# State columns side by side in `vs` from the third batch on

## The chip, the cores and the metric

One core of a Trainium2 chip runs the whole kernel in one launch. The metric is device time in microseconds of one execution; before the change it was 651.02 us, the median of 3 runs (648.34 to 651.56). The profile is of one further execution, which took 647.52 us.

## The reference

Three layers follow each other, all in float32, for 4 batches, 8 heads, 768 positions and head size 48. The first is attention with a decaying state per head, which is written as a loop over positions; the second mixes positions with angles; the third is a gated layer with a normalisation:

```python
for t in range(S):                                   # per batch and head
    state = f[:, :, t, :, None] * state + einsum('bhd,bhe->bhde', k[:, :, t], v[:, :, t])
    y[:, :, t] = einsum('bhd,bhde->bhe', q[:, :, t], state)
theta = x @ w_theta;  zr, zi = x * cos(theta), x * sin(theta)
u = x + w_tok_r @ zr + w_tok_i @ zi
x = u + maximum(u @ w_ch, 0)
h = maximum(x @ w_in, 0);  u, v = halves of h
out = (u * (w_spatial @ normalise(v) + b)) @ w_out
```

## The kernel before

The attention doesn't loop over positions. Positions are cut into NC = 12 chunks of C = 64. Two heads are worked on together, so there are 16 units (4 batches of 4 pairs), numbered u = 0 to 15; the third batch is units 8 to 11 and the fourth units 12 to 15. For each unit:

- `att_load` (line 507) brings the pair's keys (`kp`), queries (`qa`), values by position (`vn`) and, straight from the input `va`, the values by place in the chunk (`vs`, lines 523 and 524) into SBUF. `vs` has two buffers, used by even and odd units.
- `att_w` (line 529) makes each chunk's own contribution to the state (`pw`, 24 small matmuls of 64 rows by 64 columns with 48 columns moving), which ScalarE copies to `ub`; VectorE runs the decay over the chunks in one scan (line 550) into `cb`; ScalarE copies the states with two ACTIVATEs (line 553) from `cb` into the other half of `vs`, one chunk further on. In `cb` and `vs` the chunk is the innermost index, so the 48 numbers of one chunk's state row lie 12 floats apart, and so do the values that come from `va`.
- `att_s` (line 555) makes the scores inside the chunks (`psc`, 24 matmuls of 64 rows, 64 columns of weights and 64 columns moving, in two groups of 12). VectorE masks them and puts them beside the queries in `qa`.
- `att_x` (line 575), in two groups g of 6 chunks, multiplies `qa` (the weights, 128 rows by 64 columns) with the 48 columns of one chunk in `vs`: 12 matmuls a group, which go by turns to the upper and the lower half of the output partitions. ScalarE copies each group's `px` to `X`.

Float32 matmuls run as two passes, so the trace has two records for each. The second layer takes `X` through transposes (`pt`), angles (`pth`) and the position mix (`acc`, `hh`). In `mixes` (line 961) the units 4 to 15 are laid between the `acc` steps of the second layer by ticks (`UNIT`, `DECAY`, `THETA`). The third layer runs after that, one batch after the other.

The order of the instructions on each engine up to the end of the second layer is worked out by a planner (`Plan`, line 87) when the kernel is built. It gives each operation a cost (`cost`, line 96), lets each engine take the operation that can start first, by urgency, and fixes the order found. A matmul with fewer than 128 output rows is charged by line 124. GpSimd's operations keep the order of the program. The padding column of `vs` (chunk 0 has no state before it) is set to zero once, in `att_open` (lines 458 to 460).

Of the kernel before, what the change touches and what calls it, by code (L numbers as in the profile page):

```python
# [10 lines left out]
F32 = mybir.dt.float32  # L11
# [4 lines left out]
AF = mybir.ActivationFunctionType  # L16
# [5 lines left out]
P = 128  # L22
B, H, S, D = 4, 8, 768, 48
DM = H * D
NP = H // 2
C = 64
NC = S // C
# [11 lines left out]
BUFS = {"f": 1, "k": 2, "q": 2}  # L39

FILL = 30
WARM = {("s", 0, 0): 20}

HLAG, XLAG = 2, 5
# [42 lines left out]
class Plan:  # L87
# [8 lines left out]
    def cost(self, o, e, ins, out, src):  # L96
        n = max([b.n for b in out + src] or [0])
        k = type(ins).__name__
        if e == "A":
            if k == "InstActivation":  # L100
                return 0.19 + 0.84e-3 * n
            return 1.28
        if e == "V":
            if o.name.startswith("tensor_tensor_scan"):
                return 0.16 + 2.07e-3 * n
            if o.name == "tensor_scalar":
                return 0.15 + 0.53e-3 * n
            if o.name == "reciprocal":
                return 0.22
            return 0.15 + 1.045e-3 * n  # L110
        if e == "G":
            return 0.1 + 0.8e-3 * n if o.name == "memset" else 0.8
        if e == "Q":
            return ISSUE
        m, r = out[0].rows, out[0].n
        o.mode = (src[-1].rows, m)
        if o.name == "transpose":
            return 0.109
        if len(src) == 2 and src[0].t == src[1].t:
            return 0.0  # L120
        if src[0].dt == F32R:
            return max(r / 2.4 + 13.3, m / 1.2 + 2) / 1e3
        if m < P:
            return max(2 * r / 2.4, 54) / 1e3 + 0.004
        return max(2 * (2 * r / 2.4 + 2), 214) / 1e3

    def add(self, e, name, ins):
# [230 lines left out]
class Kernel:  # L358
# [70 lines left out]
    def warm(self, p, key):  # L429
        for _ in range(WARM.get(key, 0)):  # L430
            self.T.matmul(p[:, 0:P], lhsT=self.ident, rhs=self.ident, start=True, stop=True)


    def att_open(self, ctx):
        tc, V, A, G = self.tc, self.V, self.A, self.G
        self.a1 = a1 = self.pool(ctx, "a1", 1, side="left")
        self.a2 = self.pool(ctx, "a2", 2, side="left")
        self.mask = a1.tile([P, C], F32, name="mask")
        G.memset(self.mask, 1.0)
        for h in range(2):  # L440
            m = self.mask[64 * h : 64 * h + 64, :]
            G.affine_select(out=m, in_=m, pattern=[[1, C]], compare_op=ALU.is_ge, fill=0.0, base=0, channel_multiplier=-1)
        self.one = a1.tile([P, NC, C], BF16, name="one")
        G.memset(self.one, 0.0)
        G.memset(self.one[:, :, 0:1], 1.0)
        self.icp = a1.tile([P, S], F32, name="icp")
        self.cw = a1.tile([P, S], F32, name="cw")
        self.VS = [a1.tile([P, 2, D, NC], F32, name=f"vs{i}") for i in range(2)]
        self.VN = [a1.tile([P, 2, NT, D], F32, name=f"vn{i}") for i in range(2)]
        self.KP = [a1.tile([P, S + NC], F32, name=f"kp{i}") for i in range(2)]  # L450
        self.QA = [[a1.tile([P, S], F32, name=f"qa{i}{h}") for h in range(2)] for i in range(2)]
        self.KT = a1.tile([P, NT, DM + 64 - D], F32, name="kt")
        for i in range(2):
            G.memset(self.KP[i], 0.0)
            for h in range(2):
                G.memset(self.QA[i][h][64 * h : 64 * h + 64], 0.0)
        G.memset(self.KT[:, :, DM:], 0.0)
        for t in self.VS:
            G.memset(t[0:64, 0, :, 0], 0.0)
            G.memset(t[64:128, 1, :, 0], 0.0)  # L460
        self.dn, self.un = {}, {}


# [65 lines left out]
    def att_w(self, u):  # L529
        self.group()  # L530
        V, A, T = self.V, self.A, self.T
        w2 = u % 2
        KT, VN, VS = self.KT, self.VN[w2], self.VS[w2]
        if u < NP:
            cu = self.c1.tile([P, 2, D, NC], F32, name=f"cu{u}", tag=f"uT{w2}")
            cb, ub = cu[:, 0], cu[:, 1]
        else:
            cb, ub = [self.a2.tile([P, D, NC], F32, name=f"{n}{u}", tag=n, bufs=1) for n in ("cb", "ub")]
        A.activation(cb, self.KP[w2][:, None, S:].to_broadcast([P, D, NC]), AF.Copy)
        w = [self.bank("pw") for _ in range(2)]  # L540
        self.warm(w[0], ("w", u))
        w = [x[:, 0 : 6 * D].rearrange("p (n d) -> p n d", n=NT) for x in w]
        for n in range(NT):
            for s, i in ((0, 0), (1, 1), (1, 0), (0, 1)):
                o, r, h = slice(64 * i, 64 * i + 64), slice(64 * s, 64 * s + 64), 2 * (u % NP) + i
                T.matmul(w[s][o, n], lhsT=KT[r, n, D * h : D * h + 64], rhs=VN[r, i, n], start=True, stop=True)
        for s in range(2):
            A.activation(ub[:, :, s:NC:2], w[s].rearrange("p n e -> p e n"), AF.Copy)
        fl = lambda z: z.rearrange("p e c -> p (e c)")
        V.tensor_tensor_scan(fl(cb), fl(ub), fl(cb), 0.0, op0=ALU.add, op1=ALU.mult)  # L550
        for i in range(2):
            r = slice(64 * i, 64 * i + 64)
            A.activation(VS[r, i, :, 1:NC], cb[r, :, 0 : NC - 1], AF.Copy)

    def att_s(self, u, g):
        self.group()
# [18 lines left out]
    def att_x(self, u, g, X):  # L575
        self.group()
        A, T, pr = self.A, self.T, u % NP
        qa, VS = self.QA[u % 2], self.VS[u % 2]
        ps = self.bank("px")
        self.warm(ps, ("x", u, g))  # L580
        ps = ps[:, 0 : 6 * D].rearrange("p (n i d) -> p n i d", n=3, i=2)
        for i in range(2):
            for c in range(6):
                cc = 6 * g + c
                T.matmul(ps[64 * (c % 2) : 64 * (c % 2) + 64, c // 2, i, :], lhsT=qa[i][:, C * cc : C * cc + C], rhs=VS[:, i, :, cc], start=True, stop=True)
        A.activation(X[:, 3 * g : 3 * g + 3, 96 * pr : 96 * pr + 96].rearrange("p b (i e) -> p b i e", i=2), ps, AF.Copy)

    def att_pe(self, u, X):
# [432 lines left out]
    def run(self):  # L1021
# [25 lines left out]
        p = self.bank("pt")  # L1047
        for _ in range(FILL):
            self.T.matmul(p[:, 0:P], lhsT=self.ident, rhs=self.ident, start=True, stop=True)
# [57 lines left out]
def layout(inputs):  # L1107
    import numpy as np

    f32 = np.float32  # L1110
    c = np.ascontiguousarray

    def heads(x):
        return c(x.transpose(0, 1, 3, 2).reshape(B * NP, 2 * D, S))

    raw = lambda x: x.view(np.uint64) if x.dtype == np.float64 else x
    v = inputs["v"]
    v2 = v.reshape(B, NP, 2, S, D)
    tr = inputs["moe_w_tok_r"].T.reshape(NT, P, 2, TH)
    ti = inputs["moe_w_tok_i"].T.reshape(NT, P, 2, TH)  # L1120
    return {
        "q": heads(inputs["q"]),
        "k": heads(inputs["k"]),
        "f": heads(inputs["f_logit"]),
        "vt": c(v2.transpose(0, 1, 2, 4, 3).reshape(B * NP, 2, D, S)),
        "vu": c(v2.reshape(B * NP, 2, NT, P, D).transpose(0, 3, 1, 2, 4)),
        "va": c(v2.reshape(B * NP, 2, NC, C, D).transpose(0, 1, 3, 4, 2)),
        "wt": raw(c(inputs["moe_w_theta"])),
        "wc": raw(c(inputs["moe_w_ch"])),
        "tok": raw(c(np.stack([tr, ti], 0).transpose(3, 1, 2, 0, 4))),  # L1130
        "wi": raw(c(inputs["moe2_w_in"])),
        "wp": raw(c(inputs["moe2_w_spatial"].T)),
        "bs": c(inputs["moe2_b_spatial"]),
        "wo": raw(c(inputs["moe2_w_out"])),
    }
# [14 lines left out]
```

## Time and profile before

| | |
|---|---|
| median of 3 runs | 651.02 us (648.34 to 651.56) |
| the profiled execution | 647.52 us |
| its span, first to last instruction | 645.5 us |
| TensorE (PE) busy | 610.1 us |
| weight loads (PEld), beside PE | 562.9 us |
| VectorE (DVE) busy | 426.2 us |
| ScalarE (ACT) busy | 339.9 us |
| GpSimd (POOL) busy | 26.4 us |

Busy time of PE is from the start of a matmul to its modelled end, and matmuls overlap, so the time of a run of matmuls is read from the chain of waits, which counts each moment once. The chain follows the work back from the last instruction: at each step to what released it, or to the instruction before it on its engine. A row of a wait names the waiting engine and tile, an arrow, and whom it waited for.

### The profile page before, as it was taken

To read this page: it belongs to the slowest core of one execution; us is meant where nothing else is said; L and a number is where in the kernel's file an instruction comes from. 1 tells how busy PE (TensorE), PEld (TensorE's weight loads), DVE (VectorE), ACT (ScalarE), POOL (GpSimd) and SP (SyncE) were. 2 spreads that over 40 slices of the span, in tenths; PEclk is the share of its full clock that TensorE was granted. 3 is DMA by queue.
4 is the path that set the end of the run, shared out by engine and by line. 5 is a ranking of instruction groups with operands and counts; after the bars stand their busy time and mean duration, and the time that the engine had idled before them with its cause. 6 is when DMAs were issued, how large, how long until landed. Compare 5 with 4: busy or idle time off the path is not lost.

```text
span 645.5 us, 12790 instructions
## 1 busy us (share of the span) xinstructions
PE 610.1 (95%) x5140; PEld 562.9 (87%) x5140; DVE 426.2 (66%) x757; ACT 339.9 (53%) x637; POOL 26.4 (4%) x72
## 2 busy tenths in 40 slices
PE   9478987999999999999999999999999999999996
PEld 8366656786798999999999998999899989999996
DVE  4788798985999958855886625875645174518250
ACT  4567886447887658944784304733541264126211
POOL 5010001000001100010000000000000000000000
PEclk9679997799999999999999999999999999999999
DMA  8877757987858998375657635241010100020002
GB/s 264 246 220 245 273 172 221 297 283 202 293 188 293 295 276 268 99 219 193 218 187 237 240 110 159 77 145 49 25 50 24 62 13 25 1 74 1 1 1 79
DMA packets 40963, 102.05 MB, mean 158 GB/s; under 512 B 5696, under 2 KB 11840, under 8 KB 40896
## 3 DMA queue, kind: packets, MB, share of 16 engines
q1 hardware_dynamic: 40896, 101.15, 49.1%
q8 instruction: 42, 0.69, 0.5%
q14 instruction: 25, 0.20, 0.1%
HBM read 71.17 MB, written 20.45 MB: 142 GB/s over the span
## 4 chain that ended last, share of the span: by engine, by line
PE 82%; DVE 8%; DMA 3%; ACT 2%; POOL 1%; issue 1%; SPq 1%; ACTq 0%; DVEq 0%; POOLq 0%
PE acc L337 20%; PE pg L337 15%; PE pu L337 8%; PE po L337 8%; PE pv L337 8%; PE px L337 6%; PE hh L337 6%; PE pth L337 5%; PE psc L337 3%; PE pt L337 2%; PE pw L337 1%; DVE tk L337 1%; DVE icp L337 1%; DVE sn L337 1%; DVE qa L337 1%
## 5 line engine op out<-in xcount | busy, mean ns | idle before, releaser
L337 PE MATMUL acc<-tk,z 128*128 128x384 f32 x828 | 170.2, 357 | 1.2 <-DVE tk L337 1.2
L337 PEld LDWEIGHTS acc<-tk,z 128*128 128x128 f32 x828 | 144.4, 190 | 11.2 <-DVE tk L337 1.6
L337 PE MATMUL pg<-wp,vn 128*128 128x384 f32 x576 | 100.5, 334 | 0.0
L337 PEld LDWEIGHTS pg<-wp,vn 128*128 128x128 f32 x576 | 99.9, 188 | 0.0
L337 PE MATMUL pu<-x,wi 128*128 128x384 f32 x288 | 50.7, 334 | 0.0
L337 PE MATMUL po<-wo,gt 128*128 128x384 f32 x288 | 50.6, 336 | 0.0
L337 PEld LDWEIGHTS pu<-x,wi 128*128 128x128 f32 x288 | 50.1, 188 | 0.3
L337 ACT ACTIVATE gt<-g 128x384 fp32r<-128x384 f32 x32 | 16.8, 527 | 63.5 <-DVE g L337 63.5
L337 PEld LDWEIGHTS po<-wo,gt 128*128 128x128 f32 x288 | 50.0, 188 | 0.0
L337 PE MATMUL pv<-wi,x 128*128 128x512 f32 x216 | 49.8, 390 | 0.0
L337 PEld LDWEIGHTS pv<-wi,x 128*128 128x128 f32 x216 | 40.5, 188 | 8.2
L337 PEld LDWEIGHTS px<-vs,qa 128*64 128x64 f32 x768 | 36.5, 170 | 12.8 <-ACT vs L337 6.4
L337 PE MATMUL px<-vs,qa 128*64 128x48 f32 x768 | 40.6, 275 | 7.3 <-ACT vs L337 5.9
L337 DVE BATCH_NORM_STATS2 st<-vv 128x6 f32<-128x512 f32 x24 | 16.5, 692 | 42.5 <-ACT vv L337 42.5
L337 PEld LDWEIGHTS psc<-qa,kp 64*64 64x64 f32 x768 | 27.8, 145 | 19.0 <-issue 10.1
L337 PE MATMUL psc<-qa,kp 64*64 64x64 f32 x768 | 31.6, 233 | 13.1 <-DMA kp<-k 5.5
L337 PE MATMUL hh<-uT,wc 128*128 128x384 f32 x216 | 41.5, 341 | 0.7 <-DVE sn L337 0.5
L337 DVE TENSOR_TENSOR qa<-psc,mask 64x384 f32<-64x384 f32 x64 | 35.5, 555 | 8.7 <-PE psc L337 7.2
L337 PEld LDWEIGHTS hh<-uT,wc 128*128 128x128 f32 x216 | 37.4, 188 | 2.6 <-DVE uT L337 1.3
L337 DVE TENSOR_TENSOR g<-pg,bs 128x384 f32<-128x384 f32 x32 | 17.7, 557 | 27.0 <-PE pg L337 27.0
L337 ACT ACTIVATE ws<-ws 128x768 f32<-128x768 f32 (+2 forms) x28 | 20.6, 738 | 17.4 <-DMA ws<-wi_dram 7.6
L337 ACT ACTIVATE X<-px 128x288 f32<-128x288 f32 x32 | 13.1, 409 | 30.6 <-PE px L337 30.4
(111 smaller groups left out, 920.5 us busy)
## 6 DMA issues: line engine op xcount, KB each, us to landing
tk<-tkp SPq DMA_DIRECT2D x48, 384.0 KB, 4.1
ws<-tok_dram SPq DMA_DIRECT2D x12, 768.0 KB, 5.3
tkp<-tk SPq DMA_DIRECT2D x20, 384.0 KB, 4.1
f<-f_dram SPq DMA_DIRECT2D x12, 384.0 KB, 5.0
k<-k_dram SPq DMA_DIRECT2D x12, 384.0 KB, 5.6
q<-q_dram SPq DMA_DIRECT2D x12, 384.0 KB, 7.3
vn<-vu_dram SPq DMA_DIRECT2D x16, 288.0 KB, 6.9
vs<-va_dram SPq DMA_DIRECT2D x32, 144.0 KB, 4.1
```

Of the source, the lines that this page charges most:

```text
L337: r = f(*a, **k)
```

## The change

For the units from 8 on (`NEAR = 8`), `vs` holds for each chunk its 48 columns side by side; for the units 0 to 7 the chunk stays innermost as before. The tile has the same size, and `states` gives the view that fits the unit. The input `va` is laid out to match on the host, so the transfer moves the same bytes. The source of the state copy, `cb`, keeps its layout, so ScalarE's copy of units 8 to 15 writes with a jump of 48 floats. The zero column of chunk 0 lies elsewhere in the new layout and is set again by GpSimd at units 8 and 9, once for each buffer. The planner's costs are changed too: an ACTIVATE that writes with a step of more than 2 and has more than 128 elements is charged 0.95 ns an element more, and a small matmul whose moving operand has a step over 1 is charged 16 instead of 4 ns on top of its base.

```diff
+NEAR = 8
...
             if k == "InstActivation":
-                return 0.19 + 0.84e-3 * n
+                return 0.19 + 0.84e-3 * n + (0.95e-3 * n if out[0].step > 2 and n > P else 0)
...
         if m < P:
-            return max(2 * r / 2.4, 54) / 1e3 + 0.004
+            return max(2 * r / 2.4, 54) / 1e3 + (0.016 if src[0].step > 1 else 0.004)
...
-        self.VS = [a1.tile([P, 2, D, NC], F32, name=f"vs{i}") for i in range(2)]
+        self.VS = [a1.tile([P, 2, NC * D], F32, name=f"vs{i}") for i in range(2)]
...
-            G.memset(t[0:64, 0, :, 0], 0.0)
-            G.memset(t[64:128, 1, :, 0], 0.0)
+            G.memset(t[0:64, 0, 0 : NC * D : NC], 0.0)
+            G.memset(t[64:128, 1, 0 : NC * D : NC], 0.0)
...
+        if NEAR <= u < NEAR + 2:
+            for i in range(2):
+                self.G.memset(self.states(u, i)[64 * i : 64 * i + 64, 0], 0.0)
...
-            A.activation(VS[r, i, :, 1:NC], cb[r, :, 0 : NC - 1], AF.Copy)
+            vs, cs = self.states(u, i), cb[r, :, 0 : NC - 1]
+            if u < NEAR:
+                A.activation(vs[r, :, 1:NC], cs, AF.Copy)
+            else:
+                A.activation(vs[r, 1:NC].rearrange("p c e -> p e c"), cs, AF.Copy)
+
+    def states(self, u, i):
+        v = self.VS[u % 2][:, i]
+        return v.rearrange("p (e c) -> p e c", c=NC) if u < NEAR else v.rearrange("p (c e) -> p c e", c=NC)
...
-                T.matmul(..., lhsT=qa[i][:, C * cc : C * cc + C], rhs=VS[:, i, :, cc], start=True, stop=True)
+                T.matmul(..., lhsT=qa[i][:, C * cc : C * cc + C], rhs=VS[i][:, :, cc] if u < NEAR else VS[i][:, cc], start=True, stop=True)
...
+    va = v2.reshape(B * NP, 2, NC, C, D)
-        "va": c(v2.reshape(B * NP, 2, NC, C, D).transpose(0, 1, 3, 4, 2)),
+        "va": c(np.concatenate([va[:NEAR].transpose(0, 1, 3, 4, 2).reshape(NEAR, 2, C, -1), va[NEAR:].transpose(0, 1, 3, 2, 4).reshape(B * NP - NEAR, 2, C, -1)])),
```

## Rows read from the trace of the kernel before

**Rows 1.** The page's head and its busy times: us, share, instructions.

```profile
span 645.5 us, 12790 instructions
PE 610.1 (95%) x5140; PEld 562.9 (87%) x5140; DVE 426.2 (66%) x757; ACT 339.9 (53%) x637; POOL 26.4 (4%) x72
```

**Rows 2.** Stretches: engines' busy us (instructions), granted clock, DMA share, GB/s.

```profile
core 0: us, PE busy (x) PEld busy (x) DVE busy (x) ACT busy (x) POOL busy (x), PEclk, DMA share, GB/s
0.00:60.00 60.00, 41.42 (x684) 38.64 (x686) 45.16 (x63) 34.72 (x59) 14.06 (x39) 0.83 0.81 248
60.00:100.00 40.00, 34.77 (x236) 23.38 (x234) 34.87 (x50) 32.36 (x58) 1.10 (x2) 0.96 0.68 225
100.00:131.00 31.00, 27.42 (x448) 23.38 (x448) 27.04 (x36) 18.26 (x33) 3.00 (x8) 0.78 0.81 257
131.00:195.00 64.00, 63.96 (x540) 52.22 (x538) 53.79 (x78) 47.25 (x82) 0.87 (x5) 1.00 0.74 242
195.00:230.00 35.00, 33.51 (x473) 30.86 (x464) 32.24 (x43) 24.03 (x41) 4.95 (x12) 1.00 0.94 291
230.00:262.00 32.00, 32.00 (x342) 29.96 (x341) 21.96 (x36) 23.20 (x49) 0.24 (x2) 1.00 0.90 257
```

**Rows 3.** PE's waits from 131 to 391 us: total us, times, longest us.

```profile
PE psc L337 <- DVE qa L337: 1.5, 1, 1.5
PE hh L337 <- DVE sn L337: 0.5, 1, 0.5
```

**Rows 4.** Chain of waits: start us, us, engine, tile, count of records.

```profile
117.45 2.73 PE px L337 x48
...
242.08 0.84 PE pw L337 x48
...
246.02 0.84 PE psc L337 x24
...
252.59 1.18 PE px L337 x24
...
257.95 0.98 PE pt L337 x9
...
283.85 6.45 PE acc L337 x36
290.30 1.54 PE psc L337 x48
...
293.08 2.23 PE px L337 x48
```

**Rows 5.** One stretch, `px` alone: busy of PE, PEld, ACT; clock, DMA.

```profile
117.50:120.00 2.50, 2.50 (x48) 2.50 (x48) 0.41 (x1) 0.50 1.06 294
```

**Rows 6.** Groups of instructions by shape: busy us, mean ns, idle before.

```profile
L337 ACT ACTIVATE vs<-cb 64x528 f32<-64x528 f32 x24 | 15.4, 642 | 4.7 <-DVE cb L337 4.5
...
L337 ACT ACTIVATE X<-px 128x288 f32<-128x288 f32 x32 | 13.1, 409 | 30.6 <-PE px L337 30.4
...
L337 ACT ACTIVATE ub<-pw 128x288 f32<-128x288 f32 x24 | 9.1, 427 | 1.9 <-PE pw L337 1.8
...
L337 POOL MEMSET vs<- 64x48 f32 x4 | 0.7, 176 | 0.2
...
L337 POOL MEMSET kt<- 128x96 f32 x1 | 0.2, 183 | 0.1
...
L337 POOL MEMSET mask<- 128x64 f32 x1 | 0.2, 151 | 0.0
```

**Rows 7.** Timeline of ScalarE behind unit 8's copies: start us, us.

```profile
169.17 1.33 ACT L337 ACTIVATE vs<-cb 64x528 f32<-64x528 f32 x2
170.52 0.85 ACT L337 ACTIVATE z<-sn 128x768 fp32r<-128x768 f32 x1
```

**Rows 8.** Timeline around unit 15's copies and products.

```profile
298.90 1.32 ACT L337 ACTIVATE vs<-cb 64x528 f32<-64x528 f32 x2 [1.94 <-DVE cb L337]
...
300.88 2.30 PE L337 MATMUL px<-vs,qa 128*64 128x48 f32 x48
```

**Rows 9.** PE's waits before 131 us: total us, times, longest us.

```profile
PE px L337 <- ACT vs L337: 5.9, 2, 3.9
...
PE pt L337 <- DVE k L337: 4.4, 1, 4.4
```

More of the change, by code (lines that the diff above doesn't have):

```diff
@@ L577, in att_x @@
         A, T, pr = self.A, self.T, u % NP
-        qa, VS = self.QA[u % 2], self.VS[u % 2]
+        qa, VS = self.QA[u % 2], [self.states(u, i) for i in range(2)]
         ps = self.bank("px")
@@ L584, in att_x @@
                 cc = 6 * g + c
-                T.matmul(ps[64 * (c % 2) : 64 * (c % 2) + 64, c // 2, i, :], lhsT=qa[i][:, C * cc : C * cc + C], rhs=VS[:, i, :, cc], start=True, stop=True)
+                T.matmul(ps[64 * (c % 2) : 64 * (c % 2) + 64, c // 2, i, :], lhsT=qa[i][:, C * cc : C * cc + C], rhs=VS[i][:, :, cc] if u < NEAR else VS[i][:, cc], start=True, stop=True)
         A.activation(X[:, 3 * g : 3 * g + 3, 96 * pr : 96 * pr + 96].rearrange("p b (i e) -> p b i e", i=2), ps, AF.Copy)
```

## The prediction

> **What bounds the kernel now.** I read the page first: a span of 645.5 us of which TensorE (PE) is busy 610.1, VectorE (DVE) 426.2, ScalarE (ACT) 339.9 [rows 1]. Then the table by stretch [rows 2], which the reader should take in two halves. Up to 131 us PE lacks 18.6, 5.2 and 3.6 us of the stretches and its granted clock is 0.83, 0.96 and 0.78: this is an opening that waits for DMA and for the decay work on DVE. From 131 us PE is busy 63.96 of 64 us, 33.51 of 35 and 32.00 of 32 at clock 1.00. Third, what PE waits for between 131 and 391 us: the largest wait is 1.5 us for `qa`, the next 0.5 [rows 3]. So from 131 us on the kernel runs at the rate at which PE gets through its queue, and time taken out of PE's own work there comes off the end unless something else becomes late. The changed units (8 to 15, the third and fourth batch) all have their `px` products after 171 us, so in that second half. Fourth, the chain of waits gives what a run of products costs in sequence, without the overlap that busy times hold [rows 4].
>
> **The products, 16 groups of 12.** The chain has 24 instructions (12 products of two passes) of `px` in 1.18 us and 48 in 2.23, so 93 ns a product [rows 4]. `psc`, which also loads 64 weight columns for each product, also uses two tiles of the array at a time and streams 64 columns, not 48, takes 0.84 and 1.54 us; `pw`, with the same 48 columns and four tiles at a time, 0.84 us for 48 [rows 4]. `px` differs from them in two things: its moving operand is read with a jump of 12 floats (48 bytes), and its tiles are 128 rows high where theirs are 64. The second I can nearly rule out: the transposes `pt` load 128 columns over 128 rows and take 0.98 us for 9, 109 ns each, or 54 ns for 64 columns, and `acc` streams 384 columns over 128 rows, 36 in 6.45 us, 179 ns each, so 0.47 ns a column; full height slows neither the load nor the stream. A third row speaks for the read: at half the clock (0.50 from 117.5 to 120 us, so 1.2 GHz) 48 `px` take 2.73 us against 2.23 at full clock [rows 4, 5]; a run that the array's clock held would have doubled.
> Without the jump I take the `psc` rate. Six units have both groups in one run: 6 x (2.23 - 1.54) = 4.1 us. Units 8 and 12 have theirs apart: 4 x (1.18 - 0.84) = 1.4 us. Sum 5.5 us less PE work. Bounds: nothing at one end (if the jump is not the cause); at the other the `pw` rate, 8 x (2.23 - 0.84) = 11.1 us. I keep `psc`, since `px` too has only two tiles at a time. A loss on this side I exclude: the same instructions read the same number of elements, side by side.
> One rule is to be weighed. The Trainium skill (TensorE: Matmul & The Clock Gate, "The mechanism" of its part on packing) says that a weight load overlaps running matmuls only where the row groups differ, which full-height tiles never do. By it load and stream of a `px` tile would add up, and only the stream would get shorter: about half my gain, the second rival below. The trace does not agree for the transposes, at full height: 109 ns is the load of 128 columns alone, with no room for a stream of 128 columns behind it.
>
> **ScalarE's copies, 16 of them.** Two for each unit carry the states from `cb` to `vs`, 64x528 in 642 ns each [rows 6]. They read side by side as before and now write every 48th float (192 bytes apart), where before runs of 11 lay together. No row shows ScalarE writing with such a jump. Nearest on the engine: `ub` writes every second float, 427 ns for 288 elements against 409 for `X` side by side, 18 ns more, or 0.03 us for 528. Nearest in the jump: POOL's memset of `vs` writes every 12th float, 176 ns for 48 elements, while 64 side by side take 151 and 96 take 183 [rows 6]; the two latter give 55 ns fixed and 1.0 ns an element as their line, so 48 would be 135, and the jump adds 41 ns, 0.85 ns an element, or 0.45 us for 528. That is the end I take, because the jump decides and 48 bytes are nearer to 192 than 8 are; the far end is twice that, 0.9 us. Below nothing is excluded: no access gets shorter.
> So 16 x 0.45 = 7.2 us more ScalarE work, 0.9 us per unit on the way from scan to products. It is covered by the distance between the copies and the products, in which PE has `acc` work: no `px` after 131 us waits for `vs` [rows 3]. The tightest is unit 15: its copies end at 298.90 + 1.32 = 300.22 and `px` starts at 300.88 [rows 8]; 0.9 us later it is 0.25 us late, and I charge 0.3. Unit 8 has the copies from 169.17 to 170.50 and `z` right behind them [rows 7]: what queues there on ScalarE is the angle work of the next batch, 0.9 us later, and ScalarE has 16.8 us free in 131 to 195 us [rows 2]. If that cover were gone at every unit, 8 x 0.9 = 7.2 us would come back and eat the whole gain.
> The Trainium skill (SBUF — State Buffer, the note on cachelines under "Door 1") says that an access going to a new 16-byte line each time pays a penalty; it would charge both these writes now and the old `px` reads. [...]
>
> **Small parts.** Two memsets of 64x48 each at units 8 and 9, 4 x at most 176 ns on POOL [rows 6], which is busy 0.87 us of 64 there [rows 2]; they wait for the products of units 6 and 7, done tens of microseconds before; POOL's later decay steps queue behind them and see 0.35 us at most. Cost nothing. The DMA of `vs` moves the same bytes to the same rows. Units 0 to 7 keep their addresses.
>
> **What is late next.** With PE faster, DMA: its share is 0.94 from 195 to 230 us and 0.90 to 262 [rows 2], 61.7 us of 67. Units 9 to 12 save 3 x 0.69 + 2 x 0.34 = 2.75 us there; I let a quarter be lost to later landings, 0.7 us. All of it lost is a rival.
>
> **The planner.** All orders up to the end of the mixes are worked out anew: a product of the first two batches is charged 70 ns instead of 58 (their charge nears the 93 that the trace shows), each changed copy about 0.5 us more. From 131 us an order of PE work that has no waits has little to give or lose. Before 131 us the order decides what PE waits for (4.4 us for `k`, 5.9 us for `vs` [rows 9]), and I can't work out its sign; I take nothing for it in the sum and let the range reach 4.4 us to either side; more is a rival.
>
> **Sum.** -5.5 + 0.3 + 0.7 = -4.5 us. The profiled execution took 647.5 us (span 645.5 and 2.0 around it), so 643.0 for such a run; it lies under the three runs shown (648.3 to 651.6), so on their median of 651.0 I forecast 646.5.
>
> **The rivals.**
> - *DMA takes it.* The 2.75 us between 195 and 262 us are wholly lost: -5.5 + 0.3 + 2.75 = -2.5, 648.5 us. For: the shares above. Against: with them PE waited only 1.5 us.
> - *Load and stream add up.* Load 54 ns and stream 48 x 0.47 = 22 ns make 76 ns a product instead of 93: 8 x 24 x 17 ns = 3.3 us, less 1.0 of costs: 648.7 us. For: 54 and a stream at half that rate, 45, make 99, near the 93 measured. Against: the `pt` row.
> - *The jump isn't the cause.* Nothing gained, 0.3 us lost to unit 15: 651.3 us. For: `px` differs in its height too. Against: the `pt` and `acc` rows, of full height.
> - *The opening gets longer (slower).* The new order brings the wait for `k` at 98 us twice (4.4 us more), and the low clock of that stretch grows with it: clock 0.78 over 31 us is 6.8 us lost now [rows 2], two thirds of that again is 4.5. 651.0 - 4.5 + 8.9 = 655.4 us. For: only this stretch changes order with no cover. Against: the new charges differ by 0.14 us a group there. It decides from a loss of 4.5 us in the opening; measurably slower from 7.8.
> - *The opening gets shorter* by a wait of 4.4 us: 642.1 us.
>
> **How the numbers follow.** Forecast 0.50, DMA 0.12, load and stream 0.12, no cause 0.05, longer opening 0.13, shorter 0.08. About 0.5%, 3.3 us, is what can be told from no change: faster means under 647.8. The forecast's own range is 643.5 to 649.5; four fifths of it, the shorter opening and a fifth of the half gains are faster: 0.40 + 0.08 + 0.05, rounded up for the bound at the `pw` rate, 0.55. Slower 0.14: the longer opening and a little of "no cause". The rest, 0.31, is the same. The range goes from 640.5 (the shorter opening and the bound of `pw`) to 653.
>
> **What would show it.** In the new trace: 48 `px` of units 8 to 15 in about 1.54 us of the chain (93 ns still: the jump was not the cause; 76: the second rival); the 16 changed copies at about 1.1 us and the 16 others at 642 ns; no wait of `px` for `vs` after 131 us over 0.5 us; PE's waits before 131 us with the same sum, 27 us idle. A time over 649.5 us with `px` at the `psc` rate would put the fault with the planner or DMA: then the opening's idle time, or waits for `tk` from 195 to 262 us, have to show it.

## The result and the profile after

The changed kernel took 644.07 us (643.77 to 644.55, 4 runs) beside 651.29 us of the kernel before (648.34 to 654.83, 4 runs): ratio 0.9872, 95% interval [0.9847, 0.9898]. The profiled execution took 644.26 us, span 642.1. Three later comparisons of the same two kernels gave 0.9911 [0.9880, 0.9941], 0.9918 [0.9887, 0.9949] and 0.9906 [0.9870, 0.9942]. Over all four comparisons the 26 executions of the changed kernel have a median of 646.7 us, and the 72 of the kernel before 652.4: about 5.7 us or 0.9% less, against a forecast of 4.5.

The chain of waits of the changed kernel (start us, us, engine, tile, records):

```profile
100.17 2.73 PE px L339 x48
...
128.05 2.22 PE px L339 x48
...
167.90 0.84 PE px L339 x24
...
288.32 1.54 PE psc L339 x48
...
294.23 1.54 PE px L339 x48
```

Units 8 to 15 have 24 `px` in 0.84 us and 48 in 1.54, to the digit the `psc` rate, where [rows 4] had 1.18 and 2.23. Units 6 and 7, with the layout of before, still take 2.22 (128 us). The 2.73 us at 100 us belong to unit 4, also in the old layout, at a granted clock of 0.50.

The copies, from the view of the tile `vs` (count, ns minimum/median/maximum, first and last start), answer to [rows 6]:

```profile
L339 ACT ACTIVATE vs<-cb x24: 633/1146/1216, 78.4 to 301.1; 64x528 f32<-64x528 f32 x24
L339 POOL MEMSET vs<- x8: 129/154/178, 7.5 to 206.0; 64x48 f32 x8
```

Eight of the 24 are still of 0.64 us; the 16 changed ones take 1.15, 0.50 us more each. What PE waits for after 131 us, and the stretches, answer to [rows 2, 3]:

```profile
PE hh L339 <- DVE sn L339: 3.1, 1, 3.1
PE px L339 <- DVE qa L339: 0.9, 1, 0.9
PE pth L339 <- DVE xt L339: 0.8, 1, 0.8
PE pt L339 <- ACT xT L339: 0.6, 1, 0.6
```

```profile
core 0: us, PE busy (x) PEld busy (x) DVE busy (x) ACT busy (x) POOL busy (x), PEclk, DMA share, GB/s
0.00:60.00 60.00, 42.91 (x676) 39.94 (x678) 45.41 (x63) 33.60 (x58) 14.86 (x39) 0.80 0.81 248
60.00:100.00 40.00, 34.81 (x240) 23.53 (x236) 33.85 (x48) 32.93 (x58) 1.10 (x2) 0.96 0.68 216
100.00:131.00 31.00, 28.78 (x450) 24.38 (x451) 29.55 (x40) 19.07 (x35) 3.00 (x8) 0.89 0.90 280
...
195.00:230.00 35.00, 34.81 (x497) 31.89 (x497) 30.15 (x41) 25.73 (x39) 4.58 (x12) 1.00 0.97 282
230.00:262.00 32.00, 30.57 (x446) 27.67 (x441) 26.26 (x41) 26.16 (x53) 0.75 (x4) 1.00 0.87 246
```

No `px` waits for `vs` there, as forecast. But the largest wait is new, 3.1 us at 310 us. The timeline shows whose it is (start us, us, in brackets the idle time before):

```profile
310.72 0.84 ACT L339 ACTIVATE x<-xs 128x768 fp32r<-128x768 f32 x1 [3.94 <-DMA xs<-x2d]
311.47 0.47 ACT L339 ACTIVATE sn<-pth 128x384 int32<-128x384 f32 x1
...
312.47 0.55 DVE L339 SCALAR_TENSOR_TENSOR sn<-sn,pth 128x384 f32<-128x384 int32 x1
...
313.07 3.40 PE L339 MATMUL hh<-uT,wc 128*128 128x384 f32 x18 [3.08 <-DVE sn L339]
```

ScalarE stands at `x`, the third layer's load, whose transfer lands late; the angle step `sn` queues behind it on ScalarE, VectorE behind that, and PE waits for the `th` bank that VectorE reads. So this order has a weak spot that the old one had not: the three later traces of the changed kernel have the same wait with 2.6 to 3.9 us, the two traces of the kernel before 0.5 and 0.4 us.

### The profile page after: what moved, and what is told of

Same layout as the page of the kernel before. It is cut to its first block, busy times and chain, and to the rows that moved or that the text cites. A ratio compares the mean times of both kernels' runs of the same rounds, so it can differ in the third digit from the quotient of the medians.

```text
span 642.1 us, 12784 instructions
## 1 busy us (share of the span) xinstructions
PE 605.7 (94%) x5140; PEld 558.4 (87%) x5140; DVE 427.4 (67%) x757; ACT 346.0 (54%) x637; POOL 28.7 (4%) x76
## 4 chain that ended last, share of the span: by engine, by line
PE 79%; DVE 8%; DMA 5%; ACT 4%; issue 1%; POOL 1%; SPq 0%; DVEq 0%; ACTq 0%; POOLq 0%
PE acc L339 19%; PE pg L339 16%; PE pu L339 8%; PE po L339 8%; PE pv L339 8%; PE pth L339 5%; PE hh L339 5%; PE px L339 4%; PE psc L339 3%; PE pt L339 2%; DVE icp L339 2%; PE pw L339 1%; DMA f<-f_dram 1%; DMA xs<-x2d 1%; DMA tkd<-wb 1%
## 5 line engine op out<-in xcount | busy, mean ns | idle before, releaser
L339 PE MATMUL px<-vs,qa 128*64 128x48 f32 x768 | 35.5, 253 | 5.6 <-ACT vs L339 3.9
L339 PEld LDWEIGHTS px<-vs,qa 128*64 128x64 f32 x768 | 31.8, 159 | 10.2 <-ACT vs L339 4.8
L339 ACT ACTIVATE vs<-cb 64x528 f32<-64x528 f32 x24 | 23.8, 990 | 14.1 <-DVE cb L339 13.9
L339 ACT ACTIVATE sn<-sn 128x384 f32<-128x384 f32 x48 | 24.5, 516 | 7.8 <-DVE sn L339 7.5
```

Source lines behind the costliest of these rows:

```text
L339: r = f(*a, **k)
```

## The experiments

The layout and the order changed together, so the first two runs take them apart. With the charges of the planner's cost function set by unit rather than by step, its order can be kept while the layout changes, and the other way round.

**The new layout in the old order.**

```diff
-                return 0.19 + 0.84e-3 * n + (0.95e-3 * n if out[0].step > 2 and n > P else 0)
+                return 0.19 + 0.84e-3 * n
...
-            return max(2 * r / 2.4, 54) / 1e3 + (0.016 if src[0].step > 1 else 0.004)
+            return max(2 * r / 2.4, 54) / 1e3 + 0.004
```

> The new layout with the planner's charges of before; the order of all engines is that of before, but for the two pairs of memsets on POOL. Theory (the read of px was held by its jump, and the saving comes off the end): 48 px of units 8 to 15 in 1.54 us of the chain, 16 copies at 1.15 us, and 4 to 5.5 us less than before (ratio 0.992 to 0.994), since this order left no room for the longer copies. Rival (the changed order made the gain): px the same 1.54 us but the end moves by less than 1.5 us, because this order turns the time into waits of PE after 131 us.

**The old layout in the new order.**

```diff
-                return 0.19 + 0.84e-3 * n + (0.95e-3 * n if out[0].step > 2 and n > P else 0)
+                return 0.19 + 0.84e-3 * n + (0.95e-3 * n if self.far else 0)
...
-            return max(2 * r / 2.4, 54) / 1e3 + (0.016 if src[0].step > 1 else 0.004)
+            return max(2 * r / 2.4, 54) / 1e3 + (0.016 if self.strided else 0.004)
...
-        return v.rearrange("p (e c) -> p e c", c=NC) if u < NEAR else v.rearrange("p (c e) -> p c e", c=NC)
+        return v.rearrange("p (e c) -> p e c", c=NC)
...
```

`far` is set for the copies of units 8 to 15, `strided` for the `px` of units 0 to 7. In the traces VectorE and ScalarE have, record by record, the order of before in the first run and that of the changed kernel in the second; on PE a few neighbouring records change places, as between two traces of one kernel.

> The layout of before in the order of after: the planner is told after's charges unit by unit, and the order of all engines is the same as after's. Theory: 5.0 us of the changed kernel's gain is the layout, so this one takes 5.0 us more than after, some 649 us, within 0.5% of before (ratio 0.994 to 1.000); px 2.23 us for 48 everywhere. Rival (the order): within 1.5 us of after, ratio 0.987 to 0.991.

**The changed kernel beside them.** No edit.

> The changed kernel itself, to stand beside the others on one chip: 0.985 to 0.990 of before by its first runs. Theory: below e1 by the order's share, 0 to 3 us; rival (the order makes the gain): below e1 by 5 us or more.

| layout | order | median us | ratio to before |
|---|---|---|---|
| old | old | 652.91 (26 runs) | 1 |
| new | old | 650.07 (12) | 0.9948 [0.9917, 0.9979] |
| old | new | 650.43 (13) | 0.9947 [0.9925, 0.9970] |
| new | new | 646.99 (9) | 0.9911 [0.9880, 0.9941] |

By the ratios, which are not the quotients of the medians, each alone gives about 0.5%, and by the medians (2.8 and 2.5 us) the two nearly add up to the 5.9 of both. In the new order the layout is worth 650.43 - 646.99 = 3.4 us by the medians, in the old 652.91 - 650.07 = 2.8; by the ratios it is 2.4 and 3.4, so neither order is shown to suit it better. Both intervals leave out 1: the layout is not the whole gain, and the order is not either. The layout's 2.8 us lie between the expectations, under the 4 to 5.5 us named and over the rival's 1.5, and the interval, about 1.4 to 5.4 us, settles no more. The old layout in the new order has the ratio that the theory gave, but lies 3.4 us above the changed kernel and not 5.0; its rival (within 1.5 us) is refuted. The changed kernel itself came out just above the 0.985 to 0.990 named and 3.1 us below the first run, at the edge of its theory. The edits did their part: 48 `px` of unit 9, here to the modelled end of the last, in the first and the second run:

```profile
217.32 1.61 PE L339 MATMUL px<-vs,qa 128*64 128x48 f32 x48
```

```profile
219.38 2.29 PE L340 MATMUL px<-vs,qa 128*64 128x48 f32 x48
```

With the layout alone PE waits from 193 to 232 us as follows; in [rows 3] one wait of 1.5 us was all (below it the whole stretch, columns as in [rows 2]):

```profile
PE psc L339 <- DVE qa L339: 2.1, 2, 1.8
PE psc L339 <- DMA qa<-q: 1.0, 2, 0.8
```

```profile
193.00:232.00 39.00, 35.73 (x514) 32.37 (x512) 34.45 (x45) 28.77 (x43) 5.30 (x14) 0.96 0.95 276
```

The DMA share there is 0.95 and PE comes to `psc` before its operands. But the second trace of the kernel before, below, has the same two waits with 1.6 and 1.1 us, so only 0.4 to 1.6 us of the 3.1 can be put down to the layout. New is the clock: 0.96 in the stretch, where both traces of before have 1.00 from 195 to 230 us. Where the rest of the 5.5 us goes in this order is not shown.

**The kernel before once more, with its trace.** No edit.

> The kernel before, once more with its trace: its runs lie between 648 and 657 us, the profiled one took 647.5. Theory (the executions differ in the opening): 650 to 656 us, with the position mix of the second half as long as in the first trace to 1 us and the difference before 131 us, in PE's waits or the granted clock. Rival (they differ along the whole kernel): more than half of the difference after 131 us.

It took 649.95 us, 2.4 more than the first trace. Of that, 0.7 us are there by the 235th record of `acc` (193.8 us from the start against 193.1) and 1.8 by the first record of the third layer's `pv` (392.4 against 390.6); the rest lies in the third layer. PE's waits from 193 to 232 us are 2.7 us instead of 1.5, at the same place:

```profile
PE psc L337 <- DVE qa L337: 1.6, 1, 1.6
PE psc L337 <- DMA qa<-q: 1.1, 2, 0.7
```

So more than half of this difference arises after 131 us, which was the rival's sign, and the time falls just short of the theory's 650 to 656 us. One pair of traces decides little, though: the third layer alone, the same work in every kernel, took 254.7 to 257.8 us in the 14 traces. The first trace was at the fast end of that kernel's executions (647.5, where the 72 others lie between 648.3 and 656.9), and one trace locates no difference of 2 us.

**Runs of several lengths.** Units 8 to 15 hold the chunks in runs of j: products read with a jump of j floats, the copy writes runs of j.

```diff
+RUNS = [12] * 8 + [1, 2, 3, 4, 6, 12, 2, 4]
...
+        return v.rearrange("p (b e j) -> p b e j", e=D, j=RUNS[u])
...
+                A.activation(vs[r].rearrange("p b e j -> p e b j"), self.cb0[r, 0 : D * NC].rearrange("p (e b j) -> p e b j", e=D, j=j), AF.Copy)
```

> Units 8 to 15 hold the chunks in runs of 1, 2, 3, 4, 6, 12, 2 and 4: products read their 48 columns with a jump of as many floats, and ScalarE's copy writes runs as long (all 12 chunks, 64x576, from a source shifted by one). Theory (an access pays when it shares no 16 bytes with the one before it): 24 px of a group take 0.84 us at jumps 1 and 2, up to 1.18 at 4, 6 and 12, and between at 3; the copy takes 1.2 us at runs of 1, falls towards 0.68 with the length of the run and is below 0.9 at 2. Rival (any jump costs the same): 1.18 us from jump 2 on. Second rival (it grows with the jump): 4 and 6 between 0.84 and 1.18.

Timeline, products of the units with jumps 1, 2, 3, 4, 6 and 12, 2, 4 in this order (to the modelled end of the last, which is 0.07 us more than in the chain):

```profile
167.85 0.91 PE L340 MATMUL px<-vs,qa 128*64 128x48 f32 x24
220.77 1.61 PE L340 MATMUL px<-vs,qa 128*64 128x48 f32 x48
233.43 1.81 PE L340 MATMUL px<-vs,qa 128*64 128x48 f32 x48
237.53 1.26 PE L340 MATMUL px<-vs,qa 128*64 128x48 f32 x24
...
260.69 2.33 PE L340 MATMUL px<-vs,qa 128*64 128x48 f32 x48
293.44 2.29 PE L340 MATMUL px<-vs,qa 128*64 128x48 f32 x48
304.69 1.60 PE L340 MATMUL px<-vs,qa 128*64 128x48 f32 x48
312.91 2.34 PE L340 MATMUL px<-vs,qa 128*64 128x48 f32 x48
```

And their copies, two each (runs of 1, 2, 3, 4, 6):

```profile
160.07 2.47 ACT L340 ACTIVATE vs<-cb 64x576 f32<-64x576 f32 x2
216.02 1.49 ACT L340 ACTIVATE vs<-cb 64x576 f32<-64x576 f32 x2
222.72 1.62 ACT L340 ACTIVATE vs<-cb 64x576 f32<-64x576 f32 x2
229.97 1.38 ACT L340 ACTIVATE vs<-cb 64x576 f32<-64x576 f32 x2 [1.92 <-DVE cb L340]
254.78 1.39 ACT L340 ACTIVATE vs<-cb 64x576 f32<-64x576 f32 x2
```

The theory holds: at the granted clock of 1.00 that all these runs had, a read with a jump of 8 bytes costs nothing, one of 12 bytes a little (1.81 against 1.61), and from 16 bytes on all cost the same, 2.3. The write with runs of 2 costs 0.74 us for 576, runs of 4 the 0.69 of a plain copy. Pairs give the fast products almost for nothing. (The kernel as a whole took 657.94 us in its one run, in an order of its own; that time tells nothing of the layout.)

**Pairs in the new order.** The order of the changed kernel, jump 2 from unit 8. The copy moves all 12 chunks, with chunk 0 last, whose value the scan makes zero.

```diff
+RUNS = [12] * 8 + [2] * 8
...
+                A.activation(vs[r].rearrange("p b e j -> p e b j"), cb[r].rearrange("p e (b j) -> p e b j", j=j), AF.Copy)
...
+                s, j = (cc - 1) % NC, RUNS[u]
+                T.matmul(..., rhs=VS[i][:, s // j, :, s % j], start=True, stop=True)
```

> The order of the changed kernel on every engine, but from unit 8 on the chunks lie in pairs: products read every second float, the copy writes pairs (64x576, its last chunk zero). It takes away most of ScalarE's longer copies and keeps the faster products. Theory: px stays at 1.54 us for 48, the copies fall from 1.15 to 0.74 us; of the 6.6 us of ScalarE work saved little shows, 0 to 1 us less than the changed kernel beside it. Rival (the longer copies cost what the layout gained too little, 1.5 to 2 us): 1.5 us or more below the changed kernel.

> The changed kernel beside it: ratio to before 0.985 to 0.994, as in its first two comparisons. By both theories.

The copies of the kernel with pairs:

```profile
L341 ACT ACTIVATE vs<-cb x24: 665/734/768, 80.3 to 302.0; 64x576 f32<-64x576 f32 x24
```

With pairs 645.72 us, ratio 0.9896 [0.9869, 0.9922], beside 647.57 us, 0.9918 [0.9887, 0.9949] of the changed kernel. The 1.8 us between them are the rival's figure, but lie within the intervals, so what the longer copies cost is not settled by time. The stretch from the 235th `acc` record to the first `pv` took 197.3 us with pairs and 198.4, 199.9, 200.4 and 198.9 us in the four traces of the changed kernel: that points to 1 to 3 us, more than the 0.3 I charged, but single traces vary as much, and the two later kernels with pairs took 197.7 and 198.8 us.

**All 16 units: pairs, and columns side by side.** `RUNS = [2] * 16` with one charge for all products, and `NEAR = 0`; both in orders of their own.

> Pairs in all 16 units, planned with one charge for all products. Theory: eight more units save 0.69 us each where PE is the bound, but in the opening PE waits anyway, so between 1 and 4 us below the changed kernel, the order's chance of 2 to 3 us either way included. Rival (all of it comes off): 5 us or more below. Second rival (the opening is held by DMA and DVE alone): within 1 us of the changed kernel.

> The change for all 16 units (columns side by side from unit 0 on). Theory: in the opening the copies are on the way to the products (PE waited 3.9 us for vs there), so 0.9 us more for each of some four units against 0.7 saved: no better than the changed kernel, within 3 us above or below by the order's chance, and above the kernel with pairs everywhere by 2 us or more. Rival (px decides in the opening too): 3 us or more below the changed kernel.

Pairs everywhere took 656.02 us, ratio 1.0033 [1.0002, 1.0064], a miss of every expectation; side by side everywhere 650.79 us, 0.9975 [0.9953, 0.9998], 3.2 us above the changed kernel beside it, just over the 3 us of its theory, which had put it above pairs everywhere; it is 5.2 us below. In the profiled execution the first has lost its clock in the opening: 0.68, 0.93 and 0.72 in the three stretches up to 131 us, where [rows 2], with the same columns, had 0.83, 0.96 and 0.78. After that it still has 0.97 to 195 us and 0.90 to 230, where [rows 2] had 1.00.

```profile
0.00:60.00 60.00, 41.58 (x622) 38.71 (x622) 43.27 (x60) 32.81 (x55) 14.11 (x35) 0.68 0.84 247
60.00:100.00 40.00, 37.05 (x282) 26.34 (x282) 32.81 (x49) 32.74 (x58) 0.12 (x1) 0.93 0.62 194
100.00:131.00 31.00, 25.13 (x341) 21.23 (x342) 28.11 (x36) 20.03 (x34) 4.13 (x8) 0.72 0.89 269
```

**Pairs everywhere, and from unit 6, in the order of the changed kernel.** The order kept, `RUNS = [2] * 16` and `[12] * 6 + [2] * 10`.

> Pairs in all 16 units, in the order of the changed kernel on every engine; beside the kernel with pairs from unit 6 it tells what the layout does in the opening, apart from the order. Theory (pairs everywhere lost by their new order): clock 0.965 to 0.975 as in the changed kernel, 644 to 647 us, no gain from units 0 to 3, whose products run at clock 0.50 where 48 px took 2.7 to 2.8 us with and without the jump. Rival (products that finish sooner leave the array idle longer in the opening and the granted clock falls): clock 0.955 or less and 650 us or more.

> Pairs from unit 6 on in the order of the changed kernel: the two units more that run at full clock (48 px in 2.22 us at 128 and 137 us). Theory: 2 x 0.69 = 1.4 us less than pairs from unit 8, and with the shorter copies 1.5 to 3.5 us less than the changed kernel beside it, ratio to before 0.984 to 0.990. Rival (what is saved there turns into waits before unit 8): within 1 us of the changed kernel.

> The changed kernel beside them: ratio to before 0.987 to 0.994, by both theories.

647.73 us with 0.9913 [0.9876, 0.9949], 645.90 with 0.9907 [0.9878, 0.9937], and the changed kernel 646.90 with 0.9906 [0.9870, 0.9942]: the same. Pairs from unit 6 are 1.0 us below the changed kernel, as the rival said, and not the theory's 1.5 to 3.5. Pairs everywhere lie 0.7 us over their theory's range and keep the clock in this order, as it said, so that the rival (0.955 or less, 650 us or more) is refuted: 0.966 over the profiled execution where the kernel with its own order had 0.943:

```profile
0.00:60.00 60.00, 40.89 (x676) 38.20 (x678) 45.33 (x63) 34.85 (x59) 14.85 (x39) 0.77 0.83 248
```

So the lost clock came with the order, not with the layout. That profiled execution had the lowest clock of its kernel's 12 (0.943 to 0.967; 0.959 to 0.969 in the 7 of pairs in the changed kernel's order), and the lower the clock, the longer the execution in the main: 658.0 and 658.9 us at 0.943 and 0.948. But the three of the 12 with 0.965 or more still took 649.5 to 652.0 us, so the clock is not the whole of the difference. And the first units gain nothing: with pairs everywhere (own order) 48 `px` of unit 4 take as long in the chain as with the jump of 12 in the changed kernel (2.73 us at 100 us) and before:

```profile
103.39 2.76 PE px L340 x48
```

No version is shown to beat the changed kernel.

## Why the prediction was right, point by point

- **The bound.** Right in part: of the 5.5 us that left PE's work, 2.4 to 3.4 came off the end. In the new order, from unit 8's first `px` to unit 15's last, the layout saves 3.8 to 4.1 us (145.1 us with the old layout, 141.1 to 141.3 in the four traces of the changed kernel), of which 0.6 to 2.4 us are lost again by the first `pv`: the wait at 310 us is 1.9 us there with the old layout and 2.6 to 3.9 with the new. In the old order the same stretch took 131.0 us with the new layout and 131.3 and 132.6 before, so the traces show 0.3 to 1.6 us saved there. And the two changes hide each other: from the 235th `acc` record to the first `pv` the traces of the changed kernel (198.4 to 200.4 us) are no shorter than those of the kernel before (197.5 and 198.6), although seven units' products got faster there; six transposes that the new order leaves for this stretch account for some 0.7 us.
- **The products.** Right to the digit: 1.54 and 0.84 us. The rival that load and stream add up (76 ns) is refuted, and so is the one that the jump is not the cause: one kernel with several jumps shows the price from 16 bytes on and none at 8. The sum of the first had set one record's load (54 ns) and stream against a whole product, which has two records. The third row for the read, that a run held by the array's clock would have doubled at half clock, was weaker than it looked: products without a jump take 2.73 us for 48 at a granted clock of 0.50 (columns side by side everywhere, 117 us), 1.8 and not 2 times their 1.54.
- **The copies.** Forecast 1.09 us, measured 1.15. The row with the nearest jump (POOL's memset) was the right guide, the one on the same engine with a jump of 8 bytes belongs to the cheap side. (The line through the two other memsets has 87 ns fixed, not 55; the 135 and what follows from it hold.) The 0.3 us for late copies: no `px` waits for `vs` after 131 us in the changed kernel, and one of unit 14 for 0.6 us with the layout alone. The Trainium skill (ScalarE: Activation LUTs, "What ACT_TABLE_LOAD costs") gives an ACTIVATE with immediate scale and bias 186 ns + 0.833 ns an element, an estimated 626 ns for 528; the trace agrees for the copies into the old layout (642 ns) and not for those that write every 48th float (1146 ns), of which the page says nothing. The rule on 16-byte lines (the Trainium skill, SBUF — State Buffer, "Door 1") agrees with both the reads at full clock (48 in 1.54 us at 8 bytes, 2.2 to 2.3 from 16 on) and the writes (0.74 us in pairs, 1.23 with none side by side).
- **DMA next.** Too small as a term: 0.7 us charged, and 2.1 to 3.1 us of the 5.5 did not reach the end. That DMA took them is not shown: with the layout alone the waits for `qa` and its transfer at 193 to 232 us are 3.1 us, against 1.5 and 2.7 before. The rival's total of -2.5 us was nearer for the layout alone (2.8 by the medians, 3.4 by the ratio).
- **The planner.** Taken as nothing, with 4.4 us to either side; the order alone gave 2.5 us by the medians and 0.53%, or 3.5 us, by the ratio. It is the step that the sum lacked. The prediction thought of the wait for `k`, which did not get shorter (4.4 and 5.5 us before, 4.8 to 6.2 in the four traces of the changed kernel). Where the gain arises is not settled. The 235th `acc` record comes at 189.0, 188.9, 191.4 and 192.6 us in the changed kernel and at 193.1 and 193.8 before, so part of it seems to lie ahead of that record; but with the old layout in the new order, in the longest execution of that kernel (653.3 us), it comes at 192.6. One difference that goes with the order is the granted clock from 100 to 131 us, 0.89 to 0.94 in these five traces and 0.78 to 0.82 in the three of the old order; from 0 to 60 us it is the other way, 0.74 to 0.80 against 0.77 to 0.83. The later stretch with the old layout in the new order:

```profile
100.00:131.00 31.00, 25.91 (x352) 20.99 (x351) 26.95 (x37) 17.50 (x31) 2.80 (x7) 0.89 0.89 272
```

- **The sum.** -4.5 was forecast; -5.7 over all comparisons is layout some 3, order 2.5 to 3.5. The two misses, layout too high and order too low, partly cancel, so that the total came so near is in part luck. The first comparison's -7.2 us is not typical: its four runs of the changed kernel (643.8 to 644.6) lie under all 22 later ones (645.1 to 650.8), and why is not shown. The range's lower end of 640.5 does not follow from the two terms named for it, which give 636.5.

## What to carry to other kernels

Look at the jump of a matmul's moving operand as at that of any other read: compare the time of a run in the chain with one of the same weight load and no jump. Where one side must jump, let pairs lie together; here that freed the reads at nearly no cost for the writes. When a kernel's order is made by a planner, a change of charges is a second change: freeze the order, and test the two apart, before the time is put down to the edit.

## What the runs showed of the hardware

- Float32 reads by TensorE at a granted clock of 1.00 (2.4 GHz): 48 `px` in 1.54 us at jumps of 4 and 8 bytes, some 1.74 at 12, 2.2 to 2.3 from 16 on, to 48 (kernel with several jumps). At 0.50 (1.2 GHz) the jump makes no difference: 2.73 us at 4 bytes (side by side everywhere), 2.76 at 8 (pairs everywhere), 2.73 to 2.76 at 48 (kernel before).
- ScalarE writes of 64x576 floats: 1.23 us with none side by side, 0.74 in pairs, 0.69 in runs of four.
- The granted clock of the opening fell with the order of the work alone: with pairs in all units the mean over an execution was 0.943 to 0.967 in one order (12 executions) and 0.959 to 0.969 in the other (7), and the kernel in the first of them took 8.3 us more (656.02 against 647.73, in two comparisons), of which the clock explains a part.
